# Masks as a product after the exponential, transposes by DMA, and PSUM pairs given out by the planner, in a two-layer windowed-attention kernel

## The chip, the cores and the metric

The kernel runs on one core of one Trainium2 chip. The metric is the device time of one execution in microseconds (us). The core has five engines that take instructions from queues of their own: PE (TensorE, matmuls), ACT (ScalarE), DVE (VectorE), POOL (GpSimd) and SP (SyncE, which here issues nearly all DMAs). Every queue is worked off in order: an instruction whose wait isn't met holds back all that is behind it on that engine.

## The reference

Two layers, each an attention block A and a block B, over x of 2048 tokens by 512 channels in bf16, with the same weights in both layers.

```
def _A_ref(x, wqkv, wo):                       # H = 32 heads of 16 channels, window W = 256
    q, k, v = split(x @ wqkv)
    scores = q k^T * (16 ** -0.5)
    mask = (i - j >= 0) & (i - j < 256)
    p = softmax(where(mask, scores, -1e9))
    return (p v) @ wo
def _B_ref(x, w_r, w_gate, w_up, w_down):      # C = 1
    r = x @ w_r;  idx = argmax of r over the 2048 tokens
    y = (silu(x[idx] @ w_gate) * (x[idx] @ w_up)) @ w_down * sigmoid(r[idx])
    return x, with y added to the row idx
for layer in (0, 1):
    x = x + _A_ref(layernorm(x));  x = x + _B_ref(layernorm(x))
```

Block B changes one token of 2048 by a gated MLP; for all others it adds the normalized row.

## The kernel before, in words

**Tiling.** The tokens are cut into NT = 16 tiles of 128. Both layers run in one pipeline of 32 steps ("windows") T = 0 to 31; window T is tile T % 16 of layer T // 16. Four windows form a batch for the projections. A window is worked off as follows; the function is named, and its line where the profile shows one.

- `ln` (L516 to L529): bn_stats on DVE, three small POOL instructions for the scale, the normalized row XN by POOL (by ACT for the first four tiles), then `transposes` (L546): 8 PE matmuls against an identity into PSUM, and `evict_t` (L554): a DVE copy of them to XNT.
- `qk` (L584): for each quarter s of the heads (8 heads each), 16 matmuls of 512 columns give queries and keys for four tiles at once; DVE evicts them to QT (L603) and KTN (L605). `vproj` (L620, L627) makes the values.
- `kscat` (L639) and `vscat` (L648, L654): DMAs spread keys and values into block-diagonal form, KBD and VBD, so that one matmul serves four heads, each in a band of 32 partitions with 32 keys.
- `attention`: for each of four quarters s and four key blocks b of 32 keys, two score matmuls (L682) on the upper and lower half of the array write 288 queries each to a pair of PSUM banks; two more (L688) add the mask, -30000 where a query must not see the key, to the first and the last 32 queries, through a matmul of a small identity II and a mask table BM; ACT takes exp of both banks in one instruction (L696) and writes PT. Then the value matmuls (L716): 12 key blocks reach a query tile, 4 matmuls of 34 columns for each quarter and block (34 is two heads of 16 values and a 1 that sums the denominator). DVE takes the reciprocals (L729) and normalizes into ON (L734).
- `out_proj` (L546 and L554 again for ON to OT, then L750): the output projection; DVE adds the residual (L755). `mod_tile` (L771 to L792): the second layernorm, the score r of each token, and the store of the row.
- `select`, `mlp_in`, `mlp_gu`, `mlp_act`, `mlp_down`: block B, started after tile 11 of layer 0 and after tile 12 of layer 1, while the rest of the layer is still under way. `select` finds the best token in two steps: each partition's best, stored to DRAM (vcd, L834), read back by all partitions (BC, L835), and a second search on DVE (L837 to L842). Three DMAs gather the token's row. A check at the end (`late`, `count`, `final_flag`) sets FLAG if a shortcut was not allowed; a general path would then run. With this input FLAG is 0.

**PSUM.** There are 8 banks, used as pairs. Pairs 0/1 and 2/3 are for the scores, by turns; pair 4/5 (ACC) holds the value sums of one window; pair 6/7 (MISC) serves all else: both transposes, `qk`, `vproj`, `out_proj` and the MLP. Only at the start does `qk` use the others too.

**Order.** No queue is written by hand. Each operation is given to the planner `Sched` with what it reads and writes, its banks, an assumed duration (`dur`, in ns) and a due time (`prio`, in windows). `schedule` plays the operations through as a list scheduler and fixes every queue's order before the kernel is built; on the chip the queues wait for each other by semaphores. A DMA is planned with 620 ns on its queue (1300 for a gather) and 2000 ns, plus its bytes at 150 per ns, until it has landed. A multi-step projection goes through `phases`: two passes over the array's halves, where the second pass waits for the end of the first.

Of the kernel before, what the change touches and what calls it, by code (L numbers as in the profile page):

```python
# [52 lines left out]
NEG = -30000.0  # L53
# [3 lines left out]
class _Op:  # L57
    __slots__ = ("idx", "eng", "fn", "deps", "dur", "name", "is_dma", "prio", "signals", "count",
                 "dma_sem", "start", "end", "waits", "dma_extra", "force")

    def __init__(self, idx, eng, fn, deps, dur, name, is_dma, prio):
# [15 lines left out]
        self.force = None  # L77


class Sched:  # L80
# [6 lines left out]
    def __init__(self, dma_latency=2000.0, sem_latency=100.0, n_dma_slots=48):  # L87
        self.ops = []
        self.last_writer = {}
        self.readers = {}  # L90
        self.bank_state = {}
        self.dma_latency = dma_latency
        self.sem_latency = sem_latency
        self.n_dma_slots = n_dma_slots
        self.dma_ops = []
        self.base = 0.0
        self._vc_lookup = {}

    def add(self, eng, fn, reads=(), writes=(), banks=(), dur=100.0, name="", is_dma=False, prio=None, extra_deps=()):
# [13 lines left out]
        for b in banks:  # L113
# [11 lines left out]
        self.ops.append(op)  # L125
        for k in writes:
            lw[k] = idx
            self.readers[k] = []
# [6 lines left out]
    def dma(self, queue, fn, reads=(), writes=(), nbytes=0, name="", prio=None, extra_deps=(), dur=None):  # L135
# [5 lines left out]
        op.dma_extra = nbytes / 150.0  # L141
# [8 lines left out]
    def schedule(self):  # L150
        ops = self.ops
        n = len(ops)
        users = [[] for _ in range(n)]
# [7 lines left out]
        for op in ops:  # L161
            if remaining[op.idx] == 0:
                _heappush(now[op.eng], (op.prio, op.idx))
        t_eng = {e: 0.0 for e in self.ENGS}
        order = {e: [] for e in self.ENGS}
        done = 0
        while done < n:
# [33 lines left out]
            done += 1  # L201
            for u in users[i]:
                remaining[u] -= 1
                uo = ops[u]
                rt = op.end + (self.sem_latency if self.needs_wait(uo, op) else 0.0)
                if rt > ready_time[u]:
                    ready_time[u] = rt
                if remaining[u] == 0:
                    ue = uo.eng
                    if ready_time[u] <= t_eng[ue]:  # L210
                        _heappush(now[ue], (uo.prio, u))
                    else:
                        _heappush(fut[ue], (ready_time[u], uo.prio, u))
# [16 lines left out]
    def analyze(self):  # L230
# [23 lines left out]
        while done < total:  # L254
# [12 lines left out]
            assert progressed, "deadlock in schedule order (cyclic wait)"  # L267

# [31 lines left out]
    def run_engine(self, e, handle, sems, dma_sems):  # L300
# [13 lines left out]
        if e == "sp":  # L314
# [5 lines left out]
            for slot, tot in sorted(totals.items()):  # L320
                handle.wait_ge(dma_sems[slot], tot)


ACC = 4
MISC = 6
NBATCH = 4
NS1 = 11
# [8 lines left out]
class Builder:  # L336
# [16 lines left out]
    def alloc(self):  # L353
        nc = self.nc
        NT, SEQ, FF, NF = self.NT, self.SEQ, self.FF, self.NF
        self.RX = 12
        self.RK = 2
# [7 lines left out]
        self.XNT = self.sb("XNT", [128, 2, 4, 512], BF16)  # L365
        self.QT = self.sb("QT", [128, 4, SEQ], BF16)
        self.KTN = self.sb("KTN", [128, 2, 4, 256], BF16)
        self.KBD = self.sb("KBD", [128, self.RK, 4, 8, 128], BF16)
        self.VN = self.sb("VN", [128, 2, 2, 4, 8, 17], BF16)
# [7 lines left out]
        self.ONESB = self.sb("ONESB", [128, 128], BF16)  # L377
        self.ZEROB = self.sb("ZEROB", [128, 64], BF16)
        self.IDB = self.sb("IDB", [128, 128], BF16)
        self.II = self.sb("II", [128, 128], BF16)  # L380
        self.BM = self.sb("BM", [128, 2, 32], BF16)
# [15 lines left out]
        self.EQ = self.sb("EQ", [128, 128], F32)  # L397
        self.CAND = self.sb("CAND", [128, 128], F32)
        self.VC = self.sb("VC", [128, 2], F32)
        self.BC = self.sb("BC", [128, 128, 2], F32)  # L400
# [16 lines left out]
        self.VCD = nc.dram_tensor("vcd", [2, 128, 2], F32)  # L417
        self.uctr = 0
# [15 lines left out]
    def init(self):  # L434
# [12 lines left out]
        S.dma("act", lambda e: e.dma_start(self.WO[:], self.A_wo.rearrange("(kc p) n -> p kc n", p=128)), writes=["wo"], nbytes=512 * 1024, name="ld_wo", prio=-7.0)  # L447
        S.dma("act", lambda e: e.dma_start(self.WR16[:], self.B_w_r.partition_broadcast(128)),
              writes=["wr16"], nbytes=128 * 1024, name="ld_wr", prio=-6.9)
        for g in range(4, self.RX, 2):  # L450
            self.load_x(g, -6.8 + 0.1 * g)
        S.add(P, lambda e: e.memset(self.ONESB[:], 1.0), writes=["onesb"], dur=100)
        S.add(P, lambda e: e.memset(self.MHALF[:], -0.5), writes=["mhalf"], dur=60)
        S.add(P, lambda e: e.affine_select(out=self.IDB[:], in_=self.ONESB[:], pattern=[[-1, 128]], compare_op=ALU.is_equal,
                                           fill=0.0, base=0, channel_multiplier=1), reads=["onesb"], writes=["idb"], dur=300)
        S.base = -8.0
        S.add(P, lambda e: e.affine_select(out=self.M8[:], in_=self.ONESB[:, 0:8].rearrange("p (a h) -> p a h", a=2), pattern=[[-64, 2], [-16, 4]],
                                           compare_op=ALU.is_ge, fill=0.0, base=0, channel_multiplier=1), reads=["onesb"], writes=["m8"], dur=100)
# [3 lines left out]
        S.add(P, lambda e: e.memset(self.ZEROB[:], 0.0), writes=["zerob"], dur=100)  # L462
        S.add(P, lambda e: e.memset(self.II[:], 0.0), writes=["ii"], dur=100)
        S.add(P, lambda e: e.memset(self.BM[:], 0.0), writes=["bm"], dur=100)
        r = slice(0, 32)
        S.add(P, lambda e: e.affine_select(out=self.II[r, :].rearrange("p (a b) -> p a b", a=4), in_=self.ONESB[r, :].rearrange("p (a b) -> p a b", a=4),
                                           pattern=[[0, 4], [1, 32]], compare_op=ALU.is_equal, fill=0.0, base=0, channel_multiplier=-1),
              reads=["onesb"], writes=["ii"], dur=200)
        S.add(P, lambda e: e.affine_select(out=self.BM[r, 0, :], in_=self.ZEROB[r, 0:32], pattern=[[1, 32]], compare_op=ALU.is_ge,
# [1606 lines left out]
```

## Time and profile before

| | |
|---|---|
| median of 3 runs | 434.2 us (433.31 to 435.35) |
| the profiled execution | 433.42 us, of which the profile's span is 431.7 us |
| PE busy | 354.1 us, 82% of the span, 10109 matmuls |
| ACT busy | 295.8 us, 69%, of which 287.0 are the 512 exponentials |
| DVE busy | 227.5 us, 53% |
| POOL busy | 152.5 us, 35% |
| granted PE clock, mean | 0.906 |

The profile is one execution. The span reaches from its first to its last instruction; the 1.7 us between span and time lie around it. A busy share is an average over stages with different limits, so the stages have to be looked at one by one. "Idle before" is the time for which an engine stood still just before the instructions of a group, with the instruction whose end ended the wait. PEld is the loading of weights into the array, which overlaps the matmuls.

### The profile page before, as it was taken

How to read it: one execution, taken by the hardware profiler on the slowest of the kernel's cores; microseconds unless marked ns; L12 is line 12 of the kernel's file. 1: busy time of each engine (PE TensorE's matmuls, PEld its weight loads, DVE VectorE, ACT ScalarE, POOL GpSimd, SP SyncE). 2: the span in 40 equal slices, each digit the busy share in tenths (PEclk: the TensorE clock that was granted, in tenths of full speed). 3: DMA queues.
4: the chain of work that ended last, by engine and by line, in shares of the span. 5: the costliest groups of instructions: out<-in, count | busy, mean ns of one | idle time of the engine just before them, and what ended most of it. 6: DMA issues, size and time to landing. Idle time of an engine off the chain costs nothing.

```text
span 431.7 us, 22240 instructions
## 1 busy us (share of the span) xinstructions
PE 354.1 (82%) x10109; PEld 246.1 (57%) x10109; DVE 227.5 (53%) x551; ACT 295.8 (69%) x526; POOL 152.5 (35%) x373
## 2 busy tenths in 40 slices
PE   0598898799899999698699978899999998739862
PEld 0254566567666676457655556666766677517620
DVE  6773564347546655556355575466544555404441
ACT  2257788778988898765285858777988788845400
POOL 9963044324424352234314074243522132312040
PEclk9999999899999999989569999989999999956555
DMA  8704124222453233337741924423442243750600
GB/s 269 254 13 92 31 46 114 26 91 46 105 93 95 69 99 60 83 83 232 225 87 29 317 40 123 98 103 79 101 81 72 59 99 70 198 127 5 197 14 21
DMA packets 107023, 43.69 MB, mean 101 GB/s; under 512 B 82980, under 2 KB 101285, under 8 KB 106920
## 3 DMA queue, kind: packets, MB, share of 16 engines
q1 hardware_dynamic: 105432, 40.74, 36.5%
q8 instruction: 81, 1.33, 1.3%
q10 hardware_dynamic: 1488, 1.44, 1.1%
q14 instruction: 22, 0.18, 0.1%
HBM read 24.26 MB, written 13.96 MB: 89 GB/s over the span
## 4 chain that ended last, share of the span: by engine, by line
PE 53%; ACT 15%; DMA 10%; DVE 7%; SPq 6%; issue 5%; POOL 3%; DVEq 0%; ACTq 0%; POOLq 0%
ACT PT L696 14%; PE PS L584 13%; PE PS L682 11%; PE PS L716 9%; PE PS L750 7%; PE PS L620 6%; DMA vcd<-VC 4%; SPq L639 4%; PE PS L954 2%; DVE XR L755 2%; PE PS L688 2%; DMA KBD<-KTN 2%; DMA BC<-vcd 2%; PE PS L546 2%; PE PS L916 1%
## 5 line engine op out<-in xcount | busy, mean ns | idle before, releaser
L696 ACT ACTIVATE PT<-PS 128x576 bf16<-128x576 f32 (+5 forms) x512 | 287.0, 621 | 85.8 <-PE PS L688 82.4
L682 PE MATMUL PS<-QT,KBD 64*128 64x288 bf16 (+6 forms) x1024 | 146.6, 291 | 27.9 <-ACT PT L696 17.8
L716 PE MATMUL PS<-VBD,PT 64*128 64x34 bf16 x5760 | 116.2, 176 | 7.1 <-issue 4.4
L716 PEld LDWEIGHTS PS<-VBD,PT 64*128 64x128 bf16 x5760 | 97.5, 94 | 18.4 <-issue 10.2
L688 PE MATMUL PS<-BM,II 64*128 64x64 bf16 (+1 forms) x1024 | 100.5, 194 | 2.7 <-issue 2.7
L682 PEld LDWEIGHTS PS<-QT,KBD 64*128 64x128 bf16 x1024 | 52.0, 96 | 66.0 <-ACT PT L696 40.5
L777 POOL TENSOR_SCALAR RSM<-XR 128x1 f32<-128x1 f32 x32 | 9.3, 292 | 208.5 <-DVE XR L772 208.4
L584 PE MATMUL PS<-XNT,WQKV 64*128 64x512 bf16 x512 | 69.3, 396 | 3.3 <-DVE VN L627 2.2
L688 PEld LDWEIGHTS PS<-BM,II 64*128 64x128 bf16 x1024 | 52.4, 98 | 9.3 <-issue 2.2
L750 PE MATMUL PS<-WO,OT 64*128 64x256 bf16 x512 | 44.9, 300 | 2.0 <-DVE OT L554 0.7
L603 DVE CAST QT<-PS 128x512 bf16<-128x512 f32 x28 | 19.4, 692 | 48.5 <-PE PS L584 48.5
L755 DVE TENSOR_TENSOR XR<-PS,XR 128x512 f32<-128x512 f32 x32 | 22.1, 692 | 41.3 <-PE PS L750 39.9
L620 PE MATMUL PS<-WQKV,XNT 64*128 64x256 bf16 x512 | 40.4, 277 | 2.2 <-DVE XR L755 1.6
L584 PEld LDWEIGHTS PS<-XNT,WQKV 64*128 64x128 bf16 x512 | 22.0, 97 | 26.3 <-issue 4.2
L627 DVE CAST VN<-PS 128x512 bf16<-128x512 f32 x32 | 22.1, 692 | 15.3 <-PE PS L620 12.5
L750 PEld LDWEIGHTS PS<-WO,OT 64*128 64x128 bf16 x512 | 21.9, 102 | 11.4 <-DVE OT L554 2.6
L620 PEld LDWEIGHTS PS<-WQKV,XNT 64*128 64x128 bf16 x512 | 20.9, 95 | 10.7 <-DVE XR L755 3.4
L529 POOL TENSOR_SCALAR XN<-XR,RS 128x512 bf16<-128x512 f32 (+1 forms) x28 | 21.5, 769 | 10.1 <-PE PS L546 9.4
L605 DVE CAST KTN<-PS 128x512 bf16<-128x512 f32 x28 | 19.0, 678 | 10.8 <-DMA KBD<-KTN 10.8
L554 DVE COPY XNT<-PS 128x512 bf16<-128x512 bf16 x32 | 13.5, 421 | 21.2 <-PE PS L546 21.0
L734 DVE TENSOR_TENSOR ON<-PS,RD 128x256 bf16<-128x256 f32 x64 | 24.1, 414 | 0.4
L546 PE MATMUL PS<-IDB,XN 64*128 64x64 bf16 x256 | 10.0, 201 | 15.7 <-ACT XN L526 14.2
(101 smaller groups left out, 310.0 us busy)
## 6 DMA issues: line engine op xcount, KB each, us to landing
scr<-XR SPq DMA_DIRECT2D x13, 516.0 KB, 4.3
vd<-VN SPq DMA_DIRECT2D x16, 272.0 KB, 3.5
VBD<-vd SPq DMA_DIRECT2D x64, 68.0 KB, 2.8
XR<-scr SPq DMA_DIRECT2D x8, 512.0 KB, 4.4
KBD<-KTN SPq DMA_DIRECT2D x120, 32.0 KB, 2.9
MW<-in_B_w_gate_dram SPq DMA_DIRECT2D x4, 896.0 KB, 7.0
MW<-in_B_w_down_dram SPq DMA_DIRECT2D x4, 896.0 KB, 5.7
XR<-in_A_x_dram SPq DMA_DIRECT2D x8, 256.0 KB, 6.9
```

What stands on the lines that cost most here:

```text
L529: S.add("pool", lambda e: e.tensor_scalar(out=XN[:, k2, :], in0=x, scalar1=RS[:, k4, 1:2], scalar2=RS[:, k4, 2:3], op0=ALU.mult, op1=ALU.add),
L584: r = e.matmul(self.PS[:, bank + w, :], lhsT=self.WQKV[rows, j, 512 * w + 128 * s:512 * w + 128 * s + 128], rhs=XNT[rows, kb, j, :], start ...
L603: S.add("dve", lambda e: e.tensor_copy(out=self.QT[:, s, tok], in_=self.PS[:, MISC, :]), banks=[MISC], writes=["qt%d_%d" % (b % 4, s)], du ...
L620: r = e.matmul(o, lhsT=XNT[rows, kb, j, 128 * jt:128 * jt + 128], rhs=self.WQKV[rows, j, 1024 + 256 * w:1280 + 256 * w], start=(ph == 0 an ...
L627: S.add("dve", lambda e: e.tensor_copy(out=vout, in_=vin), banks=[MISC, MISC + 1], writes=["vn%d_%d" % (pr % 2, m2)], dur=650, name="evv")
L682: r = e.matmul(self.PS[:, pair + x, 0:n], lhsT=self.KBD[rows, k2, s, 4 * (T % 2) + b, :], rhs=self.QT[rows, s, q0:q0 + n], start=True, sto ...
L688: r = e.matmul(o, lhsT=self.II[rows, :], rhs=w, start=False, stop=True, skip_group_check=True)
L696: return e.activation(out=o, in_=self.PS[:, pair:pair + 2, 0:n], func=ACTF.Exp, scale=0.25)
L716: r = e.matmul(self.PS[:, ACC + x, 34 * gg:34 * gg + 34], lhsT=self.PT[rows, c:c + 128], rhs=self.VBD[rows, v3, b8, :, gg, :], start=st, s ...
L734: S.add("dve", lambda e, o=o, i0=i0, i1=i1: e.tensor_tensor(out=o, in0=i0, in1=i1, op=ALU.mult), reads=["rd%d" % t], banks=[ACC + x], writ ...
L750: r = e.matmul(self.PS[:, MISC + w, 0:256], lhsT=self.OT[rows, k2, j, :], rhs=self.WO[rows, j, 256 * w:256 * w + 256], start=(ph == 0 and ...
L755: S.add("dve", lambda e: e.tensor_tensor(out=self.xf(T).rearrange("p (x c) -> p x c", x=2), in0=self.PS[:, MISC:MISC + 2, 0:256], in1=self ...
```

## The change

- **Mask.** The mask matmuls (L688) and their tables go. The exponential runs over unmasked scores, and a product with a table MSK of zeros and ones, on PT in place, follows once for each window and quarter: 512 elements for each partition, covering four key blocks. Quarters 0 and 2 are done by DVE, 1 and 3 by POOL (`MASKP`). The value matmuls wait for the product.
- **Transposes.** XN to XNT goes by a transposing DMA on SP's queue, one for two tiles, for all but the first four tiles (14 DMAs); ON to OT by one for each window but the last two (30 DMAs). The 8 matmuls and the DVE copy of each are gone. WO is loaded with its rows in another order.
- **PSUM.** An operation names a group instead of banks. `schedule` gives a bank pair to a group when its first operation is ready, in the order of due times, with at most 2 pairs for scores and 3 for the rest (4 at the start), and the group's first matmul waits for the pair's last reader. The value sums of a window are made in four groups of one quarter each instead of one of four, so `rden` and `onorm` run four times on a quarter of the data.
- **Plan.** Costs and due times are new: latencies by engine, 2700 ns for a DMA's landing, 1250 ns on SP for a transposing DMA; projections are cut into more pieces (`parts`); scores are due a whole window ahead (`LEAD`); evictions and masks are due one window earlier (`URG`). `attention` is split into `scores` and `pv`, and `build` puts all calls into one list sorted by time.
- **Selection.** The two DMAs over DRAM ahead of the second search are replaced by two PE transposes into one partition and a DVE copy; the search then runs on one partition. A 4-byte DMA pair remains, for the check alone.
- **Smaller.** KTN gets a second buffer and VN loses one; `mlp_gu` is called for each weight chunk; SP leaves out waits at the end that it knows to be met.

```diff
@@ Sched.schedule
+        for g in self.groups:
+            own = set(g.ops)
+            for i in g.ops[1:]:
+                ops[g.ops[0]].deps |= ops[i].deps - own
+            g.left = len(g.ops)
+        pairs = [(0.0, 2 * k, ()) for k in range(4)]
...
+        def grant():
+            k = 0
+            while k < len(waiting) and pairs:
+                i = waiting[k][1]
+                g = ops[i].group
+                if held.get(g.cls, 0) >= CAPS[g.cls]:
+                    k += 1
+                    continue
+                del waiting[k]
+                held[g.cls] = held.get(g.cls, 0) + 1
+                pairs.sort()
+                t, g.bank, before = pairs.pop(0)
+                for d in before:
+                    ops[i].deps.add(d)
...
+            g = op.group
+            if g is not None:
+                g.left -= 1
+                if g.left == 0:
+                    last = [j for j in g.ops if ops[j].eng != "pe"]
+                    pairs.append((max(ops[j].end for j in g.ops), g.bank, last))
+                    held[g.cls] -= 1
+                    grant()
...
+CAPS = {"s": 2, "m": 3, "q": 4}
+LEAD = 1.0
+URG = 1.0
+MIL = 0.5
+PVL = 0.5
@@ Builder.ln
-        self.transposes(self.XN, k2, ["xn#%d" % k2], "trx")
...
+        if g >= NBATCH:
+            if j % 2 == 1:
+                dst = self.XNT[:, kb, j - 1:j + 1].rearrange("p m j q -> p (m j) q")
+                S.dma("sp", lambda e: e.dma_start(dst, self.XN[:].rearrange("p m c -> p (m c)"), transpose=True), reads=["xn#0", "xn#1"],
+                      writes=["xnt%d_%d" % (kb, j - 1), "xnt%d_%d" % (kb, j)], nbytes=256 * 1024, name="dtrx", dur=1250, prio=at)
+            return
@@ Builder.scores (from attention)
-                    for x in range(2):
-                        rows = slice(64 * x, 64 * x + 64)
-                        P = self.PS[:, pair + x, 0:W].rearrange("p (a k) -> p a k", k=32)
-                        o, w = (P[:, 0:9:8, :], self.BM[rows, :, :]) if n == W else (P[:, 0, :], self.BM[rows, 0, :])
-                        r = e.matmul(o, lhsT=self.II[rows, :], rhs=w, start=False, stop=True, skip_group_check=True)
...
+            for o, m in parts:
+                S.add("pool" if s in self.MASKP else "dve", lambda e, o=o, m=m: e.tensor_tensor(out=o, in0=o, in1=m, op=ALU.mult), reads=["msk"],
+                      writes=["pt%d_%d" % ((4 * t + b) % 12, s) for b in range(4)], dur=1100 if s in self.MASKP else 380, name="mask",
+                      prio=at + 0.19 - URG)
@@ Builder.pv (from attention)
+        S.add("dve", lambda e: e.reciprocal(out=rd, in_=acc()[:, :, :, 16]), banks=[0, 1], group=G, writes=["rd%d_%d" % (t, s)], dur=160, name="rden", prio=at - URG)
...
+        S.add("dve", lambda e: e.tensor_tensor(out=o, in0=acc()[:, :, :, 0:16], in1=rd.unsqueeze(3).broadcast_to([128, 2, 4, 16]), op=ALU.mult),
+              reads=["rd%d_%d" % (t, s)], banks=[0, 1], group=G, writes=["on#%d_%d" % (k2, s)], dur=260, name="onorm", prio=at - URG)
@@ Builder.out_proj
+        if T < 2 * self.NT - 2:
+            S.dma("sp", lambda e: e.dma_start(self.OT[:, k2], self.ON[:, k2, :], transpose=True), reads=on, writes=["ot#%d" % k2],
+                  nbytes=128 * 1024, name="dtro", dur=1250, prio=at - 0.2)
+        else:
+            self.transposes(self.ON, k2, on, "tro", self.OT[:, k2], "ot#%d" % k2)
@@ Builder.select
-        S.dma("sp", lambda e: e.dma_start(self.VCD[L], self.VC[:]), reads=["vc"], writes=["vcd%d" % L], nbytes=1024, name="vc_out")
-        S.dma("sp", lambda e: e.dma_start(self.BC[:].rearrange("p a b -> p (a b)"), self.VCD[L].rearrange("a b -> (a b)").partition_broadcast(128)),
-              reads=["vcd%d" % L], writes=["bc"], nbytes=128 * 1024, name="vc_in")
+            for c in range(2):
+                r = e.transpose(self.PS[0:1, G.bank, 128 * c:128 * c + 128], self.VC[:, c:c + 1], self.IDF[:])
...
+        S.add("pe", tr, reads=["vc", "idf"], banks=[0, 1], group=G, dur=300, name="trsel")
+        S.add(D, lambda e: e.tensor_copy(out=F[0:1, 0:256], in_=self.PS[0:1, G.bank, 0:256]), banks=[0, 1], group=G, writes=["frow"], dur=350)
@@ Builder.build
+        for T in range(NW):
+            for s in range(4):
+                ev(T + 0.22 * s - 0.3, self.scores, T, s)
+                ev(T + 0.22 * (s + 1) + 0.1, self.pv, T, s)
+            ev(T + 1.25, self.out_proj, T)
...
+        for at, _, fn, args in sorted(events, key=lambda x: x[:2]):
+            fn(*args, at)
```

## The prediction, made before the changed kernel ran

> **What bounds the kernel now.** I read the page first, parts 1, 2 and 5.
>
> ```profile
> PE 354.1 (82%) x10109; PEld 246.1 (57%) x10109; DVE 227.5 (53%) x551; ACT 295.8 (69%) x526; POOL 152.5 (35%) x373
> PEclk9999999899999999989569999989999999956555
> L696 ACT ACTIVATE PT<-PS 128x576 bf16<-128x576 f32 (+5 forms) x512 | 287.0, 621 | 85.8 <-PE PS L688 82.4
> ```
>
> PE is the busiest, and the exponential's idle time is nearly all spent waiting for the mask matmul (82.4 of 85.8 us). PE's clock halves at about 180 us and for the last 45 us: those stages have to be read apart. So next, busy time by stretch (two steady ones, the end of the exponentials, the tail; the columns are PE, PEld, DVE, ACT, POOL, then PE clock):
>
> ```profile
> 105.00:165.00 60.00, 55.69 (x1788) 40.98 (x1784) 33.54 (x79) 52.52 (x91) 24.75 (x62) 1.00 0.36 85
> 300.00:370.00 70.00, 64.78 (x2091) 47.40 (x2084) 37.61 (x88) 61.27 (x106) 24.15 (x61) 1.00 0.34 76
> 370.00:415.00 45.00, 30.37 (x984) 22.80 (x982) 16.16 (x54) 21.31 (x50) 8.32 (x21) 0.62 0.45 127
> 415.00:432.00 17.00, 7.17 (x23) 1.74 (x19) 4.72 (x16) 0.00 (x0) 2.55 (x7) 0.50 0.05 14
> ```
>
> In the steady stretches PE is 93% busy and ACT 88%: two engines near their limits, holding each other up in turn. From 370 us on neither is. What a PE instruction costs its queue is read from starts, not durations, in the timeline:
>
> ```profile
> 128.46 0.30 PE L682 MATMUL PS<-QT,KBD 64*128 64x288 bf16 x2
> ...
> 128.59 0.19 PE L688 MATMUL PS<-BM,II 64*128 64x64 bf16 x2
> ...
> 128.62 0.56 PE L716 MATMUL PS<-VBD,PT 64*128 64x34 bf16 x32
> ...
> 129.03 0.28 PE L682 MATMUL PS<-QT,KBD 64*128 64x288 bf16 x2
> ```
>
> A score pair takes 0.13 us of PE's stream, a mask pair only 0.03, 32 value matmuls 0.41. The same reading at 120 to 131 us gives 0.45 for 8 matmuls of 256 columns (L620, L750), 0.87 for 8 of 512 (L584), 0.11 for 8 transposes (L546). A window T has 16 score and 16 mask pairs, 180 value matmuls, two passes each of L584, L620 and L750 and two transposes: 2.1 + 0.48 + 2.3 + 1.74 + 1.8 + 0.22 = 8.6 us. ACT's own pace is 6.08 us for 11 exponentials at 366.94, 0.553 each, 8.85 us for 16. The starts of L755, one for each window, show what is reached: 109.59 to 176.61 us is 11.2 us a window, 259.75 to 373.74 is 10.4. So **neither engine is the bound by itself; the 1.5 to 2.3 us above ACT's 8.85 are in-order queues waiting for each other**, much of it over the single MISC pair (DVE waits 39.9 us at L755 and 48.5 at L603 for PE to fill it).
>
> The chain of waits for the end shows the selection of layer 1 and the MLP behind it:
>
> ```profile
> 372.90 11.36 DMA vcd<-VC
> 384.28 3.19 DMA BC<-vcd
> ...
> 416.60 3.16 PE PS L954 x7
> ...
> 420.67 3.16 PE PS L954 x7
> ```
>
> 14.6 us for two small DMAs; meanwhile ACT stands still 6.35 us on its one small instruction of the selection (L846), with exponentials queued behind, PE runs dry (4.7 us at L682)[...].
>
> [...]
>
> **The change part by part.**
>
> *Mask matmuls out.* 512 pairs x 0.03 = 15 us of PE stream, 0.48 a window; each exponential also starts a little earlier.
>
> *Mask products in.* 128 of 512 elements. [...] Neither is on the path by its sum: POOL goes from 153 to 224 us, DVE see below. The new thing is the wait: value matmuls of a window's own keys now stand behind exponential, product and two semaphores. On POOL a product can queue behind `mod_tile` or `ln` work (a 0.77 us row, three or four short ones), so it may be 1 to 3 us late, and behind the waiting value matmul stand the next scores, for which ACT waits. The cover is that value matmuls come due most of a window after their scores (0.22 of a window plus 0.1, scores a whole window ahead). I cost it at nothing for half of the windows, 0.3 us for the others: +5 us.
>
> *Transposes out of PE.* 58 groups x 0.11 = 6.4 us, 0.22 a window; 58 DVE copies x 0.42 = 24 us.
>
> *Transposes by DMA in.* 14 of 128x1024 and 30 of 128x512 on SP's queue. SP now issues 269 DMAs; with the 632 ns of L639's median that is 170 us, and it idles for the rest. If a transpose holds SP for the planner's 1.25 us, +55 us, covered. The planner's figure is a guide because its others are near the trace: 620 against 632, 650 for bn_stats against 678. [...] I take 1.25 to issue and some 3 to 5 us to land, as the present DMAs (2.9 to 4.4 median). A late OT holds up PE at `out_proj`; it is due 0.25 of a window or more after its values, and the planner allows 1.25 + 2.7 + 0.9 = 4.8 us for it. `kscat` and `vscat` queue behind a transpose that waits for ON; they have windows of slack.
>
> *Normalization in four.* Reciprocal and product were 0.35 + 2 x 0.41 (0.37 net), about 1.1 us a window[...]. DVE in sum: 227 - 24 + 27 + 29 = 259 us, from 6.4 to about 7.3 us of each window: still under 8.85, but fuller, so evictions queue longer.
>
> *Bank pairs by need.* No instruction costs more. It lets a projection be filled while the last is being evicted, and smaller pieces let scores in between a projection's two passes (0.67 us from start to start at L620 and L750, of which 0.45 is stream). PE's stream falls to 8.6 - 0.7 = 7.9 us a window, below ACT's 8.85, so **ACT becomes the engine to wait for**. Bounds for the window: 8.85 if all waits go, 10.0 if only the stream removed is gained (10.7 as the mean of 11.2 and 10.4, minus 0.7). I take 9.5 before the mask wait, 9.7 with it: 26 undisturbed windows x 1.0 = 26 us.
>
> *Selection.* Layer 1: 14.6 us of DMA become two transposes (0.3 us of PE at most), a copy (about 0.4) and the same short DVE steps; the three gathers stay. Stretch 370 to 415 holds 21 us of exponentials; at the steady 88% it would take 24, with the gate and up matmuls (3.0 at half clock) about 27. I take 15 of the 18 us. Layer 0 has 9.3 us for the same DMAs (172.41 to 181.7), but PE had other work there (45.8 of 55 us busy from 165 to 220): 5 us.
>
> *Tail.* In the order of the changed queues the first half of `mlp_down` stands ahead of the last `out_proj`; one block of 4.1 us (416.60 to 420.67) leaves the end: 4 us. The start is moved little: five POOL selects for MSK (0.2 to 0.3 each) against the tables dropped and half of a memset: 0.
>
> Sum: 26 + 15 + 5 + 4 = 50 us off the profiled execution's 433.4 gives 383.4; that execution stands 0.8 below the median, so **384 us**.
>
> **The rivals.**
>
> *A, ACT alone sets the pace.* All waits go and a window takes 8.9: 26 x 1.8 = 47 instead of 26, and the full 18 and some more from the clock: 433 - 78, about 356. For it: PE has 0.9 us to spare for each window. Against: today both miss their floors by 15% or more, and the queues still follow a plan made from assumed durations.
>
> *B, the waits only change places.* Products on POOL, four normalizations and a DVE some 10% fuller delay value matmuls and evictions by as much as PE saves; only selection and tail remain: 433 - 24, about 410. For it: in-order queues, POOL work 47% longer. Against: no queue but PE's and ACT's comes near 8.85 us a window.
>
> *C, SP's queue becomes the bound (slower).* [...] It decides from where 44 transposes fill SP's 264 us of room: 6.0 us each on average. Then keys and values for the next windows are late and PE waits for KBD, XNT and OT. Against: the planner's 1.25 us. Nothing in this trace excludes it.
>
> **How the numbers follow.** My forecast (350 to 404: window 8.9 to 10.0, with the bounds of the rest) 0.60, A 0.12, B 0.16, C 0.12. The range leaves out C and the outer half of A and a corner of B: 356 to 426. By about 0.5%, 2 us, a measurement of this kernel can tell a difference from none (its runs lie 433.3 to 435.4). Faster: forecast, A and all but a little of B, 0.83. Same: 0.03. Slower: C and the bad end of B, 0.14.
>
> **What would show it.** Right: no row of L688, PE around 320 us busy or less, ACT's share of the steady stretches up from 88% to 93% or so at 9.5 to 9.8 us between the residual additions, no standstill of ACT at the selection, full PE clock until shortly before the end. DVE about 260 us, POOL about 224; products near 0.42 and 1.1 us. Wrong: PE waiting for POOL's products or for OT by more than 10 us in all; transposing DMAs that take more than 6 us of SP; steady windows above 10.3 us; or a stalled selection in spite of the missing DMAs.

## The result, and the profile after

The changed kernel takes **440.5 us** (median of 4 runs, 439.2 to 441.3) beside 434.8 us for the kernel before on the same chip: a ratio of 1.013, with a 95% interval of 1.009 to 1.017. It is slower by about 6 us, where 384 us were forecast. Medians count every execution; ratios and intervals here and below leave out the slow ones, those more than 1.5% above the fastest of their kernel. The profiled execution has a span of 439.0 us against 431.7.

From the page of the kernel after (busy time and share of the five engines, granted PE clock, then groups: busy us, mean ns of one | idle before, and what ended it):

```profile
PE 337.3 (77%) x8625; PEld 221.3 (50%) x8625; DVE 251.7 (57%) x729; ACT 292.7 (67%) x526; POOL 231.6 (53%) x439
PEclk9999998999599978899569998989899997967566
L770 ACT ACTIVATE PT<-PS 128x576 bf16<-128x576 f32 (+5 forms) x512 | 283.4, 625 | 95.9 <-PE PS L761 93.9
L784 POOL TENSOR_TENSOR PT<-PT,MSK 128x512 bf16<-128x512 bf16 (+1 forms) x64 | 70.7, 1104 | 101.6 <-ACT PT L770 101.2
L847 PE MATMUL PS<-WO,OT 64*128 64x256 bf16 x512 | 48.2, 316 | 18.3 <-DMA OT<-ON 18.2
L824 DVE RECIPROCAL RD<-PS 128x8 f32<-128x8 f32 x128 | 25.3, 199 | 41.7 <-PE PS L809 35.3
L784 DVE TENSOR_TENSOR PT<-PT,MSK 128x512 bf16<-128x512 bf16 (+1 forms) x64 | 27.1, 424 | 18.4 <-ACT PT L770 18.1
L826 DVE TENSOR_TENSOR ON<-PS,RD 128x128 bf16<-128x128 f32 x128 | 36.4, 286 | 2.0
```

The sums of work are near those of the forecast, PE's apart: the mask row is gone, DVE stands at 252 us (259 forecast), POOL at 232 (224), products at 0.42 and 1.10 us, but PE at 337 (320 or less forecast). Yet the exponential (L770, before L696) now waits for PE 93.9 us, not 82.4. Less work and more waiting: the order has to tell why. The wait that had no counterpart before stands at L847, the output projection (L750 before, with 2.0 us of idle time in all): 18.2 us of PE's idle time end with the landing of OT.

The stretches that were shown for before (PE, PEld, DVE, ACT, POOL busy, PE clock, DMA share):

```profile
105.00:165.00 60.00, 47.45 (x1290) 31.57 (x1287) 32.95 (x94) 44.49 (x77) 32.86 (x64) 0.86 0.63 129
300.00:370.00 70.00, 57.85 (x1618) 38.73 (x1612) 39.25 (x111) 54.34 (x95) 35.55 (x64) 0.93 0.63 116
370.00:415.00 45.00, 33.89 (x1120) 25.85 (x1119) 24.45 (x91) 30.46 (x66) 21.23 (x39) 0.77 0.53 151
415.00:439.00 24.00, 10.33 (x178) 5.58 (x178) 8.74 (x29) 0.48 (x2) 6.10 (x15) 0.64 0.06 19
```

In the steady stretches ACT works 44.5 of 60 and 54.3 of 70 us, where before it worked 52.5 and 61.3; the PE clock there is 0.86 and 0.93 in place of 1.00, and the DMA engines are filled to 0.63 instead of about 0.35. From 370 us on there is more work at a better clock (0.77 for 0.62), in part because the changed kernel is further behind there: the residual of T = 28 starts at 396.5 us, at 373.7 before.

The starts of the residual addition (L755 before, L852 after), one for each window, give the balance by part. "No DMA" is the kernel with both transposes back on PE, which comes below:

| us of the profiled execution | before | after | no DMA |
|---|---|---|---|
| start to the residual of T = 0 | 51.3 | 56.1 | 56.0 |
| T = 0 to 16 | 198.4 | 202.1 | 190.5 |
| T = 16 to 26 | 107.0 | 113.6 | 106.5 |
| T = 26 to 31 (selection of layer 1) | 59.1 | 54.7 | 50.0 |
| from there to the end | 15.9 | 12.4 | 11.6 |

So the parts with the selection and the tail gain 4.4 and 3.5 us; the start loses 4.8, and the 26 windows that were to gain 26 us lose 10.

**How OT makes PE wait.** Two lines of the answer on tile OT (SP's instruction: shortest, median, longest ns; then issue to landing in us):

```profile
L835 SPq DMA_TRANSPOSE OT<-ON x30: 1197/1313/2590, 49.1 to 397.9; - x30
DMA to landing us min/median/max: 2.4/3.6/9.1
```

The transfer holds SP for 1.3 us and lands after 3.6, as forecast, but with a tail to 9.1. One of two 9.1 us cases (the other was issued at 225.54, also behind two weight loads; PE's wait for it ended at 234.60), in the timeline (start, us, engine, line, operation, count, [idle before <- releaser]); two MLP weight loads of 0.9 MB each had been issued at 143.74:

```profile
145.13 2.59 SPq L835 DMA_TRANSPOSE OT<-ON  x1
...
147.76 3.91 SPq L608 DMA_TRANSPOSE XNT<-XN  x1
...
149.46 0.30 PE L761 MATMUL PS<-QT,KBD 64*128 64x288 bf16 x2
...
154.30 1.03 PE L847 MATMUL PS<-WO,OT 64*128 64x256 bf16 x8 [4.54 <-DMA OT<-ON]
...
155.12 0.45 PE L761 MATMUL PS<-QT,KBD 64*128 64x288 bf16 x2
...
155.61 0.65 ACT L770 ACTIVATE PT<-PS 128x576 bf16<-128x576 f32 x1 [5.12 <-PE PS L761]
```

Read it from below: ACT stands still 5.12 us for a score pair that itself waits for nothing but stands behind L847 on PE's queue; L847 waits 4.54 us for OT. Afterwards the score pair takes 0.45 us instead of 0.30: the clock has halved (1.00 granted until 151 us, 0.50 from 152 to 158). Not each of the ten waits for OT goes with a halved clock: around those of 0.42, 2.39 and 0.89 us that end at 163.94, 234.60 and 349.31 it is 1.00.

A second way to be late, on SP's queue (first column: start; second: us held):

```profile
105.26 6.69 SPq L721 DMA_DIRECT2D KBD<-KTN  x6
112.00 1.31 SPq L835 DMA_TRANSPOSE OT<-ON  x1
113.36 0.58 SPq L730 DMA_DIRECT2D vd<-VN  x1
113.99 2.11 SPq L835 DMA_TRANSPOSE OT<-ON  x1
116.86 1.31 SPq L736 DMA_DIRECT2D VBD<-vd  x3
```

The ON of the first of these transfers was normalized by 105.2 us (its last L826 started at 104.87); its transfer left at 112.0, after six KBD transfers. PE then waited 1.70 us for it, until 116.26. Read in this way, the ten transfers that PE met too early needed 6 to 14 us from the end of the last L826 to the landing, where the plan had allowed 4.8: for five the longer part passed on SP's queue ahead of the issue (up to 11.3 us), for the other five between issue and landing.

### The profile page after: what moved, and what is told of

The parts are those of the page before. It is cut to its first block, busy times and chain, and to the rows that moved or that the text cites. A ratio compares the mean times of both kernels' runs of the same rounds, so it can differ in the third digit from the quotient of the medians.

```text
span 439.0 us, 19634 instructions
## 1 busy us (share of the span) xinstructions
PE 337.3 (77%) x8625; PEld 221.3 (50%) x8625; DVE 251.7 (57%) x729; ACT 292.7 (67%) x526; POOL 231.6 (53%) x439
## 4 chain that ended last, share of the span: by engine, by line
PE 40%; ACT 20%; DVE 15%; DMA 14%; issue 5%; POOL 2%; SPq 2%; DVEq 0%; POOLq 0%
ACT PT L770 20%; DMA OT<-ON 12%; PE PS L658 11%; PE PS L847 8%; PE PS L761 8%; PE PS L809 7%; PE PS L700 4%; DMA XR<-in_A_x_dram 2%; DVE XR L852 2%; DVE QT L682 2%; DVE KTN L684 2%; DVE ST6M L868 1%; PE PS L1066 1%; DVE VN L709 1%; DVE JUNK L870 1%
## 5 line engine op out<-in xcount | busy, mean ns | idle before, releaser
L770 ACT ACTIVATE PT<-PS 128x576 bf16<-128x576 f32 (+5 forms) x512 | 283.4, 625 | 95.9 <-PE PS L761 93.9
L809 PE MATMUL PS<-VBD,PT 64*128 64x34 bf16 x5760 | 116.8, 178 | 16.0 <-issue 10.8
L809 PEld LDWEIGHTS PS<-VBD,PT 64*128 64x128 bf16 x5760 | 109.0, 95 | 35.6 <-issue 14.2
L784 POOL TENSOR_TENSOR PT<-PT,MSK 128x512 bf16<-128x512 bf16 (+1 forms) x64 | 70.7, 1104 | 101.6 <-ACT PT L770 101.2
L658 PE MATMUL PS<-XNT,WQKV 64*128 64x512 bf16 x512 | 80.5, 402 | 3.8 <-DVE MV L589 1.7
L847 PE MATMUL PS<-WO,OT 64*128 64x256 bf16 x512 | 48.2, 316 | 18.3 <-DMA OT<-ON 18.2
L852 DVE TENSOR_TENSOR XR<-PS,XR 128x512 f32<-128x512 f32 x32 | 22.1, 690 | 53.5 <-PE PS L847 51.9
L700 PE MATMUL PS<-WQKV,XNT 64*128 64x256 bf16 x512 | 47.1, 289 | 3.1 <-issue 1.4
L824 DVE RECIPROCAL RD<-PS 128x8 f32<-128x8 f32 x128 | 25.3, 199 | 41.7 <-PE PS L809 35.3
L847 PEld LDWEIGHTS PS<-WO,OT 64*128 64x128 bf16 x512 | 24.7, 105 | 28.2 <-DMA OT<-ON 20.9
L784 DVE TENSOR_TENSOR PT<-PT,MSK 128x512 bf16<-128x512 bf16 (+1 forms) x64 | 27.1, 424 | 18.4 <-ACT PT L770 18.1
L826 DVE TENSOR_TENSOR ON<-PS,RD 128x128 bf16<-128x128 f32 x128 | 36.4, 286 | 2.0
L682 DVE CAST QT<-PS 128x512 bf16<-128x512 f32 x28 | 19.3, 688 | 20.3 <-PE PS L658 20.1
L870 DVE SCALAR_TENSOR_TENSOR JUNK<-XR,WR 128x512 bf16<-128x512 f32 x32 | 25.0, 780 | 0.0
L588 DVE BATCH_NORM_STATS2 ST<-XR 128x6 f32<-128x512 bf16 (+1 forms) x32 | 20.8, 668 | 3.4 <-DMA XR<-in_A_x_dram 3.0
## 6 DMA issues: line engine op xcount, KB each, us to landing
XR<-in_A_x_dram SPq DMA_DIRECT2D x8, 256.0 KB, 10.4
```

Source lines behind the costliest of these rows:

```text
L658: r = e.matmul(self.PS[:, G.bank + w, :], lhsT=self.WQKV[rows, j, 512 * w + 128 * s:512 * w + 128 * s + 128], rhs=XNT[rows, kb, :, j, :], ...
L682: S.add("dve", lambda e: e.tensor_copy(out=self.QT[:, s, tok], in_=q()), banks=[0], group=G, writes=["qt%d_%d" % (b % 4, s)], dur=612, nam ...
L700: r = e.matmul(o, lhsT=XNT[rows, kb, jt, j, :], rhs=self.WQKV[rows, j, 1024 + 256 * w:1280 + 256 * w], start=(ph == 0 and j == 0), stop=(p ...
L770: return e.activation(out=o, in_=self.PS[:, G.bank:G.bank + 2, 0:n], func=ACTF.Exp, scale=0.25)
L784: S.add("pool" if s in self.MASKP else "dve", lambda e, o=o, m=m: e.tensor_tensor(out=o, in0=o, in1=m, op=ALU.mult), reads=["msk"], writes ...
L809: r = e.matmul(self.PS[:, G.bank + x, 34 * a:34 * a + 34], lhsT=self.PT[rows, c:c + 128], rhs=self.VBD[rows, v3, b8, :, 2 * s + a, :], sta ...
```

## The experiments

Times are medians; ratios are to the kernel before on the same chip, with 95% intervals. Differences between two experiments are ratios subtracted and taken of 436 us, a usual median of the kernel before in these runs.

| kernel | us | ratio (95%) |
|---|---|---|
| changed kernel | 440.5 | 1.013 (1.009 to 1.017) |
| ON transposed on PE | 426.2 | 0.974 (0.967 to 0.981) |
| XN transposed on PE | 433.6 | 0.992 (0.989 to 0.995) |
| both on PE ("no DMA") | 417.6 | 0.958 (0.952 to 0.963) |
| no DMA, order shifted by chance | 415.3 | 0.956 (0.950 to 0.962) |
| projection later | 430.8 | 0.988 (0.983 to 0.993) |
| no DMA, projection later | 414.1 | 0.951 (0.945 to 0.957) |
| plan told 3.6 us | 436.9 | 1.004 (1.001 to 1.007) |
| weights from ACT's queue | 446.9 | 1.023 (1.014 to 1.032) |
| products all on DVE | 446.8 | 1.026 (1.020 to 1.032) |
| no DMA, masks by matmul | 422.9 | 0.968 (0.963 to 0.973) |
| no DMA, one pair for each kind | 425.8 | 0.978 (0.973 to 0.982) |
| the same, one normalization | 426.4 | 0.977 (0.972 to 0.983) |
| no DMA, one normalization | 477.5 | 1.099 (1.091 to 1.106) |
| no DMA, three score pairs | 425.4 | 0.973 (0.969 to 0.977) |
| the same, projection later | 429.6 | 0.982 (0.977 to 0.987) |
| before, new selection alone | 428.1 | 0.984 (0.979 to 0.990) |

**1. Transposes back on PE: ON, XN, both.** The theories: (1) the transposing DMAs cost the time, (2) the mask products do, (3) the scheduler's pairs and due times do.

```diff
-        if T < 2 * self.NT - 2:      # out_proj, for ON
+        if T < 0:
-        if g >= NBATCH:              # ln, for XN
+        if g < 0:
```

ON alone: 

> The changed kernel with the transposes of ON back on TensorE and VectorE for all 32 tiles (each 0.11 us of PE's stream and a 0.42 us copy); those of XN stay with the DMA. Theory 1, the OT transfers cost the time: PE's 18.2 us of waits for OT go, and with them the scores that stand behind each wait[...]; 400 to 418 us. Theory 2, the mask products and their waits cost it: 434 to 441 us, since those stay. Theory 3, the scheduler's bank pairs and due times cost it: the waits only move, 430 to 441 us.

XN alone: 

> The changed kernel with the transposes of XN back on TensorE and VectorE; those of ON stay with the DMA. Theory 1 in the form that only OT matters (XNT is due windows later): 436 to 443 us. Theory 1 in the form that transposes by DMA slow the other transfers and SP's queue: 415 to 430 us. Theories 2 and 3: 436 to 443 us, with some us more for 28 copies of 0.42 us on VectorE.

Both: 

> The changed kernel with no transposing DMA at all: mask products, normalization in four, bank pairs by the scheduler and the new selection stay. Theory 1: 398 to 418 us, as with ON's transposes alone or a little below. Theories 2 and 3: 430 to 441 us.

Measured 426.2, 433.6 and 417.6 us. The last is just inside theory 1's range; the first two lie between the ranges. With no transposing DMA the change is a gain of 4.2%. The DMAs cost 0.055 of 436, **24 us**: given back singly, ON's are worth 17 us and XN's 9. ON's part was expected at 22 to 40 us and is smaller; XN's was expected at nothing or at 10 to 25 and lies between. PE's waits for XNT were 1.8 us in all with ON on PE, so XN's 9 us are not in waits for XNT itself; in the kernel with XN alone on PE, those for OT fall from 18.2 to 11.9. In the page and the waits of the kernel without transposing DMAs:

```profile
PE 327.1 (79%) x9089; PEld 222.7 (54%) x9089; DVE 274.4 (66%) x787; ACT 291.9 (70%) x526; POOL 231.2 (56%) x439
L770 ACT ACTIVATE PT<-PS 128x576 bf16<-128x576 f32 (+5 forms) x512 | 282.4, 624 | 75.4 <-PE PS L761 73.0
L847 PE MATMUL PS<-WO,OT 64*128 64x256 bf16 x512 | 40.1, 274 | 1.5 <-DVE OT L628 0.5
```

PE has 464 instructions more than after and is busy 10 us less: the clock is back (0.927 in the mean, 0.883 after), L847 takes 274 ns instead of 316 and waits 1.5 us in all. ACT waits 21 us less for scores. DVE has 23 us more to do, and it costs nothing that shows.

**2. Why the transfers cost: asked for too early, or too many.** One line each: the projection due later, with and without the transfers; the plan told the median landing; the weights on another queue.

```diff
-            ev(T + 1.25, self.out_proj, T)
+            ev(T + 1.6, self.out_proj, T)
-    def __init__(self, dma_latency=2700.0, ...       # another kernel
+    def __init__(self, dma_latency=3600.0, ...
-        self.S.dma("sp", lambda e: e.dma_start(dst, src), ..., name="ld_mw"    # a third, load_mlp
+        self.S.dma("act", lambda e: e.dma_start(dst, src), ..., name="ld_mw"
```

> The changed kernel with the output projection due 0.35 of a window later (T + 1.6 in place of T + 1.25); ON and XN are still transposed by DMA. If the transfers cost time because OT lands after PE has reached the projection, about 4 us more room takes most of the 18.2 us of waits away: 424 to 432 us. If they cost it by filling the queue of SP and the DMA engines, whenever PE asks for OT: 436 to 443 us.

> No transposing DMA, and the output projection due at T + 1.6 in place of T + 1.25. With the transfers this was worth about 10 us although PE's waits for OT stayed at 18.2 us. If a later projection is of use whatever transposes ON: 406 to 412 us. If it is of use only against late transfers: 415 to 421 us.

> The changed kernel, ON and XN transposed by DMA, with the plan told that a DMA lands 3.6 us after its issue (the median that the OT transfers took) in place of 2.7. If the plan's optimism puts the projection too early on PE's queue: 424 to 434 us, with fewer waits for OT than 18.2 us. If the waits come from single late landings (up to 9.1 us behind 1.8 MB of weights, or behind five to eight KBD transfers on SP's queue), which no fixed figure covers: 436 to 443 us.

> The changed kernel, ON and XN by DMA, with the 12 loads of MLP weights (0.9 MB each) issued from ACT's queue in place of SP's. If the two OT transfers that took 9.1 us stood in the ring of SP's queue behind 1.8 MB of weights: no landing of OT above about 6 us, PE's waits for OT down from 18.2 us by some 5 to 7, the time 430 to 437 us. If they were late because the 16 DMA engines were filled, whichever queue the weights came from: landings of 8 us and more stay, 437 to 444 us.

Measured: 430.8 us with the projection later, so 11 us better and in the first range; but its reason fails, since PE's waits for OT stay. The waits of this kernel (PE for OT: us in all, times, longest) and its exponentials:

```profile
PE PS L847 <- DMA OT<-ON: 18.2, 9, 6.2
L770 ACT ACTIVATE PT<-PS 128x576 bf16<-128x576 f32 (+5 forms) x512 | 281.4, 626 | 79.8 <-PE PS L761 76.4
```

They come from the profiled execution, which at 424.9 us was the fastest of six. ACT's idle time before the exponentials is 79.8 us in it, 95.9 in the changed kernel: so PE's waits for OT, summed, do not tell what they cost. The same edit without the transfers gives 2.8 us, within the intervals, at 414.1 us between its two ranges. More room is thus of use with the transfers, but not by removing PE's waits for OT; by what way it shortens ACT's these runs don't say.

With the plan told 3.6 us the median, 436.9, is about 4 us better than the changed kernel's, at the edge of the second range. The profiled execution, here too the fastest (431.6 us, of 22), has fewer waits, as the first expectation had it:

```profile
PE PS L847 <- DMA OT<-ON: 10.7, 4, 5.9
```

So this run does not decide between the two; the four waits that are left still reach 5.9 us.

With the weights on ACT's queue the late landings stay. Of that kernel, the answer on OT, and PE after the weights of layer 0:

```profile
DMA to landing us min/median/max: 2.4/3.5/8.8
151.10 1.03 PE L847 MATMUL PS<-WO,OT 64*128 64x256 bf16 x8 [3.30 <-DMA OT<-ON]
```

That transfer was issued at 142.77, behind two weight loads that left at 140.28 on the other queue: 8.3 us. So the weights' place on SP's queue is not what makes it late. Of the two causes expected, that leaves the DMA engines: in the changed kernel the packets of queue q1 take 123.9% of the time of 16 engines from 143 to 155 us, and 1.8 of their 2.5 MB are weights. PE's waits for OT are 19.3 us here. That the whole is some 4 us slower still, above both ranges, is within the intervals; its cause is open.

**3. The mask products.** All on DVE in the changed kernel; and, without transposing DMAs, the mask matmuls of before put back.

```diff
-        self.MASKP = (1, 3)
+        self.MASKP = ()
+                    for x in range(2):     # the other kernel, in scores: as in before, with II and BM
+                        r = e.matmul(o, lhsT=self.II[rows, :], rhs=w, start=False, stop=True, ...)
```

> The changed kernel with all mask products on VectorE at 0.42 us, none on POOL at 1.10 us. POOL falls by 71 us of work, VectorE rises by 27 us (252 to 279 us). Theory 2, late products on POOL hold up value matmuls and the scores behind them: 415 to 430 us. Theory 1: 434 to 443 us, the waits for OT stay at 15 to 20 us. Theory 3: 434 to 443 us.

> No transposing DMA, and the masks added by 512 pairs of matmuls as in the kernel before, not multiplied in; normalization in four, bank pairs by the scheduler and the new selection stay. To be set against the same kernel with products (417.6 us). If the matmuls taken away were worth 0.48 us a window as forecast and the products are hidden: 428 to 433 us. If the products' waits (VectorE 0.42, POOL 1.10 us ahead of a value matmul) give back what PE gains: 413 to 421 us. If they cost more than they save: below 413 us.

All on DVE costs 6 us more (1.026 against 1.013), more than any theory expected, so POOL's 1.10 us products are not what holds the kernel up. Masks by matmul cost 4.5 us more than products (0.968 against 0.958, intervals that nearly touch), so the products save time on the whole; theory 2 falls. They are worth about 5 us, not the 10 to 15 expected, and the figure lies between the first two ranges.

**4. Bank pairs.** One pair each for values and for projections, as before; or three pairs for scores.

```diff
-CAPS = {"s": 2, "m": 3, "q": 4}
+CAPS = {"s": 2, "m": 1, "a": 1, "q": 4}      # value groups of class "a"
+CAPS = {"s": 3, "m": 3, "q": 4}              # the other two kernels
```

> No transposing DMA, and as in the kernel before one pair of banks for projections and transposes and one for the value matmuls, beside two for scores. To be set against the same kernel with up to three pairs for both kinds together (417.6 us). If the pairs by need are what gains: 425 to 440 us, with VectorE and PE waiting for each other at the projections again. If they gain nothing: 414 to 421 us.

> No transposing DMA, and up to three bank pairs for scores in place of two (four pairs in all, as before). ACT still waits 73 us for scores and PE 16 us for a pair that ACT has to free. If two pairs of scores are too thin a store, so that each queue waits for the other: 400 to 411 us. If the waits come from PE being held up elsewhere for longer than a third pair covers, or the pair is missing elsewhere: 414 to 425 us.

> The same with the output projection due at T + 1.6. If the two knobs act on different waits: some 3 us below the kernel with three score pairs alone. If they act on the same wait: within 3 us of it or of 414.1 us.

425.8 us with fixed numbers: pairs by need are worth 8.6 us. Three pairs for scores give 425.4, worse by 6.5; with the projection later as well, 429.6, which no theory expected. A thin store of scores is not what holds the windows up. That the third pair is missed by the projections is likely, but not shown.

**5. Normalization in four.** Without transposing DMAs, one reciprocal and two products for a window.

```diff
+        if s == 0:
+            self.PVG, self.PVF = S.group("m"), None     # one group for a window, not one for each quarter
+        G, first = self.PVG, self.PVF
+            for i in () if g.cls == "a" else g.ops[1:]:  # second kernel: class "a", outside the grouping rule
```

> No transposing DMA, and the values of a window gathered in one bank pair and normalized once (one reciprocal, two products) as in the kernel before, not in four parts: about 0.9 us a window or 29 us less on VectorE (272 to about 245 us), while one pair stays held for a whole window. To be set against 417.6 us. If the four normalizations fill VectorE so that evictions come late: 408 to 414 us. If VectorE has room, as forecast, 415 to 421 us; if the pair held longer counts more, 422 to 430 us.

> The kernel with no transposing DMA and one pair each for projections and for values (425.8 us), and now with the values of a window normalized once, as in the kernel before. The scheduler makes the first instruction of a group wait for what all of the group waits for; here the value group is taken out of that rule, which made the last try (477.5 us) hold the first value matmul of a window until its last product. If four normalizations fill VectorE: 415 to 422 us. If VectorE has room, as forecast: 423 to 429 us. If four small groups let values be normalized earlier and that counts: 430 to 440 us.

The first took 477.5 us and missed its aim: in `schedule` the first instruction of a group waits for all that the group waits for, so a window's first value matmul waited for its last product. The second leaves that rule out for value groups. The first lines of the page, one pair for each kind, with four normalizations and then with one:

```profile
PE 332.8 (79%) x9089; PEld 226.8 (54%) x9089; DVE 272.0 (64%) x787; ACT 290.8 (69%) x526; POOL 226.9 (54%) x439
```

```profile
PE 332.5 (79%) x9089; PEld 224.8 (53%) x9089; DVE 254.8 (60%) x627; ACT 291.4 (69%) x526; POOL 226.1 (53%) x439
```

17 us of DVE gone, and 425.8 and 426.4 us: DVE has room for the four normalizations, to within some 2 us. (The second kernel's executions last 2.2 to 4.3 us longer than their spans, the first's 1.7 or 1.8; by spans alone the second is some 2 us ahead, still outside the range for a full DVE.)

**6. The selection alone,** put into the kernel before, and **a control** in which one planned duration is shifted.

```diff
-        S.dma("sp", lambda e: e.dma_start(self.VCD[L], self.VC[:]), ...)     # select, in the kernel before
-        S.dma("sp", lambda e: e.dma_start(self.BC[:]..., self.VCD[L]...), ...)
+                r = e.transpose(self.PS[0:1, MISC, 128 * c:128 * c + 128], self.VC[:, c:c + 1], self.IDF[:])
-        S.add("pe", tr, ..., dur=220, name=name)      # control, in transposes
+        S.add("pe", tr, ..., dur=240, name=name)
```

> The kernel before with the selection of the changed one alone: two transposes and a copy in place of the DMA to DRAM and back (9.3 us in layer 0, 14.6 us in layer 1). If the forecast's 15 + 5 us for it hold: 412 to 418 us. If the end is set by something else behind it (residual, weights, the last windows of values): 425 to 435 us.

> The kernel with no transposing DMA again, with one figure of the plan changed: a group of transposes on PE is planned at 240 ns instead of 220. No instruction is added or taken away; only the order on the queues may shift. It shows how much time an order shifted by chance is worth: 414 to 421 us if 1% differences between the other experiments can be read, outside of that if they can't.

The selection alone is worth 7 us (ratio 0.984, so 4 to 9), not 20; at 428.1 us it lies in the second range, that of something else behind it. Its windows T = 26 to 31 take 56.1 us in place of 59.1, and ACT's small instruction there waits for nothing; but windows 16 to 26, where nothing was edited, take 110.8 in place of 107.0. The control moves the total by 0.2% only (415.3 and 417.6 us, intervals overlapping), but in its profile windows 16 to 26 also shift, from 106.5 to 109.8, and others shift back. By this one shift totals some 1% apart can be read, though one shift does not show how far others would go, and differences of 4 to 5 us stay at the limit. A part of the span 3 us apart can't be read.

**The best version** of these is the changed kernel with all transposes on PE and the projection due at T + 1.6: 414.1 us, 4.9% below the kernel before (ratio 0.951, 0.945 to 0.957).

## Why the prediction was wrong, point by point

- **Transposes by DMA, costed at nothing on the path: this step failed, at 24 us.** Its parts were right (1.25 us on SP forecast, 1.3 measured; 3 to 5 us to land, 3.6 measured; 24 us of DVE saved, 24.6 measured). Wrong was that the median was set against the slack. The plan allowed 4.8 us; transfers behind KBD's on SP's queue or behind MLP weights in the DMA engines needed up to 14 from values to landing. PE met 10 of 30 too early, all of them past 6 us, for 18.2 us, and its queue, and so ACT, stood behind each. The forecast named this as what would make it wrong (over 10 us of PE waits for OT), but gave it no price; its one rival in this direction, C, came to late OT only through the time that a transfer holds SP. How the 24 us arise is shown in part: the late OT and what stands behind it are in the trace, but the kernel with the projection later regains 11 us with the same 18.2 us of waits.
- **26 windows at 1.0 us each: the second failed term.** Mask products (about 5 us) and bank pairs (8.6) together bring some 13, and without the transposing DMAs 8.4 us show in windows 0 to 26, nearly all of it in layer 0. The mean of 10.4 to 11.2 us that I started from hid that windows 20 to 28 ran at 9.65 already (296.57 to 373.74). (That mean is also 10.8, not the 10.7 of the working, a slip of 0.1 us a window.) Taking work off PE there left them as long (9.96 us without transposing DMAs): in the stretch 300 to 370 PE is busy 57.2 of 70 us without transposing DMAs and 64.8 before, so the stream did get shorter, but ACT did not become the engine to wait for (56.8 of 70 busy, 61.3 before). What holds these windows is open: three score pairs, one normalization or products on DVE alone do not free them (10.9, 9.6 and 11.9 us for these windows; the last was tried only with the transfers in). In all, without the transfers 8.4 us come in the 26 windows, 9.1 at the selection of layer 1 and 4.3 at the end, and the start loses 4.7: 17 us of the 50 forecast.
- **Selection, 15 + 5 us.** ACT's standstill (6.35 us) went as forecast; alone it brings 7 us in both layers together. I priced the stretch as if its 15 us were free to be used.
- **Tail, 4 us: right.** 3.5 us; the first half of `mlp_down` does stand ahead of the last projection, and only one block is left behind it.
- **Start, 0 us:** 4.8 us lost, with and without the transposing DMAs (56.1 and 56.0 us to the first residual). The first loads of x land in 10.4 us, 6.9 before; whether that is the cause is open.
- **Normalization in four, +29 us of DVE, covered: right.** 61.7 us for 35.4, and no cost when it is taken back. A reciprocal takes 0.20 us and a product 0.29; neither was shown at this size before.
- **Mask products: right in size, and not late on POOL.** One takes 0.42 us on DVE and 1.10 on POOL (L784); the trace before has no product of this form, so the size was not shown when it was forecast. Among the waits of PE in the kernel after no POOL product is named, and moving POOL's share to DVE costs 6 us.
- **Rivals.** C (SP's queue filled) falls by 1.3 us held against its 6.0; what a transfer would hold was not shown before. A falls: ACT waits longer than before, and still 75 us without the transfers. B, waits that change places with only selection and tail left (410), is what the kernel without transposing DMAs comes near to, by luck in part: it also had a DVE some 10% fuller hold PE up (by the working's own sums it is 14%), and DVE has room. With them it lacked the term that decided. Of the signs, those on the sums of DVE, POOL and the products came true, and that on ACT's standstill; PE at 320 us or less (337 came, 327 without the transfers), ACT at 93% (74 and 78% came), PE's full clock and windows at 9.7 us (13.3 from T = 6 to 11, 11.4 from 16 to 26) did not.

## What to carry to other kernels

A transfer put in place of an engine's work is priced by its late landings (here 9.1 us), not by its median (3.6): add what stands ahead of it on the issuing queue and in the DMA engines, compare with the slack in front of the in-order queue that asks for it, and count what is queued behind. When the sums of busy time come out as planned and the time doesn't, look for the row whose idle time has a new releaser. And split a mean over windows by stage before multiplying it: where windows already run shorter than the mean there may be less to take.

## What was not expected of the hardware

- The transposing DMAs of twice the width, from SBUF to SBUF, took no longer in the median: 128x512 in bf16 holds SP for 1.31 us and lands after 3.6 (2.4 to 9.1), 128x1024 holds it for 1.28 and lands after 3.5 (3.1 to 8.9).
- PE can stand still with no releaser that the profile shows. In the chain of waits of the kernel after, three neighbouring pieces (start, us, what):

```profile
411.09 0.25 PE PS L809 x17
411.34 5.33 issue
416.67 0.40 PE PS L809 x15
```

The gap lies inside a run of value matmuls, after 17 of 32 of them; DVE and POOL had ended their products, and 1.8 MB of MLP weights, issued at 407.15, were landing. Such waits are 10.8 us in all at L809 after, and 13.6 without transposing DMAs. The DMA view points to PE's own instructions. Queue q8 carries only packets of 16 KB that the profile marks "instruction", 81 before, with 10109 matmuls on PE, and 70 after, with 8625. From 411.4 to 414.2 us there is none, and the weights' queue fills the engines; from 414.2 to 415.4 there is one:

```profile
q1 hardware_dynamic: 889, 0.89, 100.6%
...
q1 hardware_dynamic: 266, 0.25, 61.2%
q8 instruction: 1, 0.02, 5.0%
```

It ended at 415.25, and PE went on 1.4 us later. In the traces of all 18 kernels PE has 173 waits of over 0.3 us without a releaser (from 60 us on); 171 of them end 1.2 to 1.7 us after the end of such a packet, while only about one in ten of all PE's matmuls start at such a time. So PE most likely waited for instructions that came late. No run tests this; the kernels with and without transposing DMAs have these waits alike.
